# A pool of five PSUM banks, first inverses by quarters, and an order planned in both directions, in a DeltaNet kernel with a mixture-of-depths block

## The chip, the cores and the metric

The kernel runs on one core of a Trainium2 chip. Its time is the time of one execution on the device in microseconds (us); smaller is better. TensorE (PE in the profile) multiplies matrices and writes only to PSUM; VectorE (DVE), ScalarE (ACT) and GpSimd (POOL) work element by element, and SyncE (SP) issues most of the DMAs. [...]

## The reference

Attention block: batch 4, 8 heads, 768 steps, head width 48. For each batch and head a state of 48x48 starts at zero, and per step, with k normed:

```
y[t]   = q[t] @ state
v_old  = state^T @ k[t]
state += beta[t] * outer(k[t], v[t] - v_old)
```

The heads' outputs side by side are x, of 4 x 768 x 384. Mixture of depths: score = x @ w_gate; in each batch the 128 rows with the highest score get `x + sigmoid(score) * (relu(x @ w1) @ w2)`, with w1 of 384x1024 and w2 of 1024x384; the other rows stay x.

## The kernel before, in words

**Chunks.** The recurrence is done in chunks of C = 64 steps. Two batches form a group, so a unit holds 16 pairs of batch and head; 12 chunks by 2 groups give 24 units, numbered i. Inside a chunk the recurrence becomes a triangular system, whose inverse is needed once for each unit and head.

**Preparation of a unit** (`prep`): k and q are loaded, turned by TensorE (`turn`, L460), copied out by ScalarE (L464), then the products k k^T (`products_g`, L479) and q k^T (`products_p`, L489) are made and copied out (L496, L503; each product lies in two banks and is copied in two parts), and `mask_p` (L511, POOL) masks the second.

**Elimination** (`eliminate`), once for four units (a set e, 0 to 5): the 64x64 triangle of each head is two 32x32 blocks on the diagonal and one below. VectorE turns the diagonal blocks so that each partition holds one whole block of 1024 elements (`turn_in`, L580), scales it, ScalarE copies it to PSUM (`fill`, L615), and 30 steps of two instructions each (`step`, L624 multiplies, L628 subtracts) invert it; then `final` (L634), `turn_out` (L640) and `turn_back` (L646). `join` puts the two inverted blocks and the block below together with two TensorE products per unit, z (L691) and j (L703), and copies on ScalarE (L697, L709).

**Recurrence of a unit** (`recur`), the serial part: V (`mm_v`, L755) puts v into PSUM through the identity; R (`mm_r`, L741) adds state times k; ScalarE copies it (L759); W (`mm_w`, L767) applies the inverse; ScalarE copies the two halves (L772); S (`mm_s`, L780) updates the state in its own bank and ScalarE copies it (L786). Outputs: Q (`mm_q`, L796) and Y (`mm_p`, L807), copied in two parts (L814), stored, weighed (L824) and summed to scores (L830).

**Depths** (`depths`), once per batch: ranks by comparison, chosen rows gathered by an indirect DMA, first product (`mm_1`, L1051), second (`mm_2`, L1065), an indirect DMA that adds into the output (L1074). Their products stand after the last W in the order of TensorE.

**PSUM.** Eight banks: three single ones called inv (turned k and q, products, z, j, Y, depths), two for the elimination (pa), a fixed pair `prec` that V, R and W of all units share, one for the state (psta).

**Order.** `Plan` holds each piece of work as an `Op` with an engine, an assumed duration, what it waits for and which buffers (rings) it takes and gives back. `order` walks forward in assumed time and lets the engines pick; `rank` runs it once and then sets each priority to the length of the tail behind the piece. `fill` puts short bf16 matmuls of ones (`filler`, L1161; one call issues two) where it thinks TensorE would stand idle. The result fixes each engine's sequence when the program is built.

Of the kernel before, what the change touches and what calls it, by code (L numbers as in the profile page):

```python
# [17 lines left out]
HC = 32  # L18

# [6 lines left out]
class Plan:  # L26
# [30 lines left out]

    def pick(self, free, ops):
# [3 lines left out]
        for t, op in sorted(ops, key=lambda x: (x[1].prio, x[1].seq)):  # L62
            at, need = max(free, t), {}
            for name, _ in op.take:
                need[name] = need.get(name, 0) + 1
            if kept & set(need):
                continue
            late = {n: sorted(self.rings[n])[k - 1] for n, k in need.items()}
            held = [n for n in late if late[n] > at]
            if held and t <= free + 0.3 and held == ["inv"]:  # L70
                kept.add("inv")
            at = max([at] + list(late.values()))
            if at < float("inf"):
                cand.append((at, op))
# [40 lines left out]
    def order(self):  # L115
# [6 lines left out]
        while len(done) < len(self.ops):  # L122
# [10 lines left out]
            for name, key in op.take:  # L133
                slots = self.rings[name]
                k = min(range(len(slots)), key=lambda x: slots[x])
                slots[k] = float("inf")
                self.slot[key] = (name, k)
# [17 lines left out]
    def rank(self):  # L155


        slots, refs = {n: len(s) for n, s in self.rings.items()}, dict(self.refs)
        self.order()
        givers, then, held, tail = {}, {}, {}, {}  # L160
# [3 lines left out]
        for op in sorted(self.ops, key=lambda o: (o.start, o.seq)):  # L164
            for name, key in op.take:
                if name != "inv":
                    for g in givers.get(held.get(self.slot[key]), []):
                        then.setdefault(g.seq, []).append(op)
                    held[self.slot[key]] = key
        for op in sorted(self.ops, key=lambda o: (o.end, o.seq), reverse=True):  # L170
            tail[op.seq] = op.dur + max(
                [tail[u.seq] + (op.lat if u.eng != op.eng else 0.0) for u in op.users] +
                [tail[u.seq] + 0.15 for u in then.get(op.seq, []) if u.seq in tail] + [0.0])
        for op in self.ops:
            hot = op.prio < -500 and op.eng != "PE"
            op.prio = -tail[op.seq] - (1000 if hot else 0)
            op.left, op.start, op.end = len(op.deps), None, None
        self.refs, self.slot = refs, {}
        for n, c in slots.items():
            self.rings[n] = [0.0] * c  # L180
# [18 lines left out]
def kernel(  # L199
# [63 lines left out]
    KF = F // P  # L263
    PSUM = bass.MemoryType.PSUM
# [21 lines left out]
    ring("a", 2, [HC * HC])  # L286
# [6 lines left out]
    ring("cmp", 2, [22 * P], BF16)  # L293
# [3 lines left out]
    rings["inv"] = [psum.tile([P, 512], FP32, name=f"inv{m}") for m in range(3)]  # L297
    plan.ring("inv", 3)
    rings["A"] = [psum.tile([P, HC, HC], FP32, name="pa")]
    plan.ring("A", 1)  # L300
    prec = psum.tile([P, 2, 512], FP32, name="prec")
    pfull = psum.tile([P, 512], FP32, name="psta")
    psta = pfull[:, :GI * 2 * D].rearrange("p (r d) -> p r d", d=2 * D)

# [41 lines left out]
    later = sbuf("later", [C])  # L346
    base = sbuf("base", [NT])
# [20 lines left out]
    wbd = [sbuf(f"wbd{m}", [GP, 2, D]) for m in range(2)]  # L368
    sts = [sbuf(f"s{m}", [GI, 2, D]) for m in range(2)]
# [6 lines left out]
    def constants():  # L376
# [10 lines left out]
        for t in wbd:  # L387
            nc.vector.memset(t, 0.0)
        for t in rings["tt"]:
# [8 lines left out]
    def late_constants():  # L398
# [4 lines left out]
        for b in range(B):  # L403
# [7 lines left out]
            nc.gpsimd.tensor_copy(tok[b][:, :, 0, 1], own[b])  # L411

# [43 lines left out]
    def turn(i, nm):  # L456
# [6 lines left out]
        def out():  # L463
            nc.scalar.copy(got(nm + "T", i),  # L464
                           got("inv", i, nm).rearrange("p (r t) -> p r t", t=P))
# [28 lines left out]
    def split_g(i, rt):  # L494
        def emit():
            nc.scalar.copy(  # L496
                blocks(got(*gk(i // BC)), i % BC)
                .rearrange("p (k r) x t -> p k r x t", r=2)[:, :, rt], small(i, "g", rt))
        return emit

    def split_p(i, rt):
        def emit():
            nc.scalar.copy(  # L503
                got("p", i).rearrange("p (r b) t -> p r b t", b=2)[:, :, rt],
                small(i, "w", rt).rearrange("p a b t -> p (a b) t"))
# [22 lines left out]
    def shift0(i):  # L528

        def emit():  # L530
            left, right = lower(got(*gk(i // BC)), slice(i % BC * GP // 2,
                                                         (i % BC + 1) * GP // 2))
            for x in range(2):
                nc.vector.tensor_copy(right[lo[x]], left[lo[x]])
        return emit

    def prep(i):
# [3 lines left out]
        for nm in "kq":  # L541
            n["l" + nm] = moved(sp, 1.3, 1.15, load(i, nm), prio=u - 30 + (nm == "q") * 34,
                                take=[(nm, i)], lat=2.5)
        for nm in "kq":
# [5 lines left out]
            n["e" + nm] = act(0.6, put, [n["t" + nm]], v, give=[("inv", i, nm)])  # L550
        for w, v, made, deps, rate in (
                ("g", u, (products_g, split_g), [n["ek"], N[e * BC].get("g")], 1.2),
                ("w", u + 31, (products_p, split_p), [n["ek"], n["eq"]], 1.2)):
            keys = [("inv", i, w, rt) for rt in range(2)]
            n[w] = pe(0.71 if w == "g" else 0.5, made[0](i), deps + [N.get(i - 1, {}).get(w)], v, rate=rate,
                      take=keys + ([("p", i)] if w == "w" else
                                   [gk(e)] * (i % BC == 0)))
            for rt in range(2):
                n[w, rt] = act(0.37, made[1](i, rt), [n[w], n.get((w, 0))], v,
                               give=[keys[rt]])  # L560
        n["mp"] = pool(1.1, mask_p(i), [n["w", 0], n["w", 1], N["masks"]], 10 * i - 10)
        done = [n["g", 0], n["g", 1]]
        if i < BC:
            n["sh"] = dve(0.6, shift0(i), done, u)
# [5 lines left out]
    def eliminate(e):  # L570
# [3 lines left out]
        eng, on = (nc.vector, dve) if e == 0 else (nc.gpsimd, pool)  # L574

        def rows(t):
            return t.rearrange("p (i c) -> p i c", c=HC)

        def turn_in():
            nc.vector.transpose(  # L580
                out=rows(got("a", e)).rearrange("p t (n x) -> p t n x", x=2),
                in_=got(*gk(e))[:, :, HC:].rearrange("p n t x -> p t n x"))

        def square():
            eng.tensor_scalar_max(nrm[:, 0], got("a", e)[:, ::HC + 1], 1e-30)
# [17 lines left out]
        def clear():  # L603
            a = rows(got("a", e))
# [3 lines left out]
        def scale():  # L608
            a = rows(got("a", e))
            eng.tensor_tensor(out=a, in0=a, op=ALU.mult,  # L610
                              in1=bh[e % 2][:, :, None].to_broadcast([P, HC, HC]))
            eng.memset(got("a", e)[:, ::HC + 1], -1.0)

        def fill():
            nc.scalar.copy(got("A", e), rows(got("a", e)))  # L615

        def step(j):
            w = HC - 1 - j

            def emit():  # L620
                a = rows(got("a", e))
# [10 lines left out]
        def final():  # L632

            nc.vector.tensor_tensor(  # L634
                out=got("a", e).rearrange("p (i c x) -> p i x c", c=HC, x=2),
# [3 lines left out]
        def turn_out():  # L639
            nc.vector.transpose(  # L640
                out=got("tt", e)[:, :, HC:].rearrange("p n t x -> p t n x"),
                in_=got("a", e).rearrange("p (i c x) -> p i x c", c=HC, x=2))

        def turn_back():
# [3 lines left out]
                in_=got("a", e).rearrange("p (i c x) -> p c i x", c=HC, x=2))  # L648
# [16 lines left out]
        last = on(1.4 if e == 0 else 2.2, scale, [s["sc"], cl], -650 if e else u)  # L665
        last = act(1.0, fill, [last], -600, take=[("A", e)])
        for j in range(1, HC - 1):
            emit, dur = step(j)
            last = dve(dur, emit, [last, N.get(("e", e - 1), {}).get("tb")], u)
        s["fi"] = last = dve(1.25, final, [last], u, give=[("A", e)])  # L670
        s["to"] = last = dve(1.3, turn_out, [last], u, take=[("tt", e)])
        s["tb"] = last = dve(1.3, turn_back, [last], u, give=[("a", e)])
        for m in range(BC):
            s["mv", m] = pool(0.7, move(m), [s["to"]], -640)
        for m in range(BC):
            join(e, m)

    def join(e, m):
# [32 lines left out]
        n["z"] = pe(0.53, z, [s["to"]], u, rate=0.3, take=[key[0]])  # L711
        n["ez"] = act(0.4, ez, [n["z"]], u, give=[key[0]])
        n["j"] = pe(0.53, jj, [n["ez"], s["tb"]], u, rate=0.3, take=[key[1]], give=[gk(e)])
# [5 lines left out]
    def recur(i):  # L719
# [5 lines left out]
        wb, s_old, s_new = wbd[i % 2], sts[(i + 1) % 2], sts[i % 2]  # L725
        both_r = prec[:, :, :GP * D // 2]
# [8 lines left out]
        def mm_r():  # L735
            t = got("kT", i)
            pr = both_r.rearrange("p r (k b d) -> p r k b d", b=2, d=D)
# [454 lines left out]
```

## Time and profile before

| what | value |
|---|---|
| median of three runs | 314.7 us (313.43 to 322.67) |
| the profiled execution, its own time | 316.69 us |
| its span, first to last instruction | 314.9 us |
| mean granted TensorE clock | 0.933 of full speed |
| busy: PE, DVE, ACT, POOL | 280.6, 201.7, 176.1, 149.1 us |
| first W (unit 0), last W (unit 23) | start at 58.0 and 250.1 us |

A time in the profile is counted from the start of its span. A line of a timeline gives start, duration, engine, source line, operation, output and inputs with their sizes, count, and in brackets how long the engine stood idle before and who ended that. A line of the stretches gives, for one stretch of the span, its length, then each engine's busy time with its count of instructions, the granted clock of TensorE and the share of time in which the DMA engines worked. A product of two float32 operands is recorded as two passes, so 16 products show as x32.

### The profile page before, as it was taken

What the parts mean: (1) busy time and instruction counts of PE and PEld (TensorE: products, weight loads), DVE (VectorE), ACT (ScalarE), POOL (GpSimd) and SP (SyncE); (2) the same over time, 40 slices, a digit from 0 to 9 for tenths busy, and PEclk for the clock granted to TensorE, in tenths of its full rate; (3) what the DMA queues carried; (4) which work ended last, traced back from release to release, by engine and by line L of the source; (5) the groups of instructions that cost most, each with busy time, mean ns of one, the idle gap of its engine ahead of it and who ended that gap; (6) DMA issues with size and microseconds to landing.
All of it is one profiled execution on the core that took longest, in us unless ns stands there. A gap on an engine that the chain in (4) does not pass through costs nothing.

```text
span 314.9 us, 15794 instructions
## 1 busy us (share of the span) xinstructions
PE 280.6 (89%) x6930; PEld 230.8 (73%) x6930; DVE 201.7 (64%) x632; ACT 176.1 (56%) x453; POOL 149.1 (47%) x232
## 2 busy tenths in 40 slices
PE   5979539998999989989999898999999999999990
PEld 5868428777888768877878677777877877777770
DVE  7379966997799779997984259957335565642000
ACT  1766406666868768676568557775467851212210
POOL 7056687834744694377042974466133442212201
PEclk9997957999999999997589999998599999999996
DMA  5776797265425343566223532435210211112012
GB/s 102 140 132 121 163 167 160 42 123 108 98 58 113 89 93 75 97 126 168 54 53 76 103 80 55 104 81 151 48 34 11 61 41 49 11 41 27 25 25 25
DMA packets 87923, 26.21 MB, mean 83 GB/s; under 512 B 82448, under 2 KB 87280, under 8 KB 87856
## 3 DMA queue, kind: packets, MB, share of 16 engines
q1 hardware_dynamic: 86256, 23.54, 35.1%
q0 software_dynamic: 1600, 1.68, 3.3%
q8 instruction: 54, 0.88, 1.1%
q14 instruction: 13, 0.11, 0.1%
HBM read 18.38 MB, written 5.51 MB: 76 GB/s over the span
## 4 chain that ended last, share of the span: by engine, by line
PE 65%; DVE 11%; ACT 8%; issue 5%; DMA 5%; POOL 3%; SPq 1%; POOLq 1%; DVEq 0%; ACTq 0%
PE inv L807 5%; PE inv L1051 5%; PE inv L460 5%; PE psta L780 5%; PE inv L1065 5%; PE prec L755 5%; PE prec L767 4%; PE psta L1161 4%; PE inv L796 4%; PE inv L703 4%; PE prec L741 3%; PE inv L691 3%; DVE pa L628 3%; DVE tmp L624 3%; PE inv L489 3%
## 5 line engine op out<-in xcount | busy, mean ns | idle before, releaser
L624 DVE TENSOR_TENSOR tmp<-a,pa 128x30 f32<-128x30 f32 (+9 forms) x180 | 58.6, 326 | 17.1 <-ACT pa L615 11.4
L628 DVE TENSOR_TENSOR pa<-pa,tmp 128x30 f32<-128x30 f32 (+9 forms) x180 | 60.8, 338 | 6.2
L824 POOL TENSOR_TENSOR xw<-x,wg 128x384 f32<-128x384 f32 x23 | 23.1, 1002 | 42.1 <-ACT x L814 23.8
L511 POOL TENSOR_TENSOR p<-p,later 128x512 f32<-128x512 f32 x24 | 30.3, 1271 | 16.2 <-ACT p L503 15.7
L731 POOL TENSOR_TENSOR v<-v,nnT 128x384 f32<-128x384 f32 x24 | 19.9, 829 | 34.1 <-DMA v<-in_v_dram 30.3
L1161 PE MATMUL psta<-warm 128*128 128x128 bf16 x242 | 27.7, 241 | 3.8 <-DVE psta L385 3.8
L772 ACT COPY wbd<-prec 64x384 f32<-64x384 f32 x48 | 22.7, 472 | 13.9 <-PE prec L767 12.5
L1051 PEld LDWEIGHTS inv<-xeT,w_sb 128*128 128x128 f32 x192 | 24.0, 192 | 5.1 <-ACT xeT L1045 0.9
L1065 PE MATMUL inv<-w_sb,hT 128*128 128x384 f32 x64 | 25.4, 498 | 0.3 <-ACT hT L1058 0.3
L1051 PE MATMUL inv<-xeT,w_sb 128*128 128x128 f32 x192 | 25.3, 279 | 0.2 <-ACT xeT L1045 0.2
L780 PE MATMUL psta<-wbd,k 128*48 128x96 f32 x352 | 20.3, 261 | 5.2 <-ACT wbd L772 4.9
L460 PE MATMUL inv<-ident,q 128*128 128x128 f32 x96 | 16.7, 307 | 7.7 <-DMA q<-in_q_dram 7.7
L807 PE MATMUL inv<-wbd,p 128*64 128x96 f32 x384 | 23.0, 267 | 0.2 <-POOL p L511 0.2
L479 PE MATMUL inv<-kT 48*64 48x64 f32 x768 | 20.2, 230 | 2.9 <-ACT g L496 2.6
L1161 PEld LDWEIGHTS <-warm 128*128 128x128 bf16 x242 | 17.5, 107 | 6.8 <-issue 2.6
L780 PEld LDWEIGHTS psta<-wbd,k 128*48 128x48 f32 x352 | 15.8, 129 | 8.7 <-ACT wbd L772 8.1
L1058 ACT ACTIVATE hT<-inv 128x256 f32<-128x256 f32 x16 | 6.1, 383 | 26.5 <-PE inv L1051 26.5
L479 PEld LDWEIGHTS inv<-kT 48*64 48x64 f32 x768 | 16.2, 140 | 6.3 <-ACT g L496 3.8
L709 ACT COPY tt<-inv 32x256 f32<-32x256 f32 x48 | 18.5, 385 | 4.2 <-PE inv L703 3.3
L755 PE MATMUL prec<-v,ident 128*128 128x192 f32 x88 | 20.7, 360 | 0.0
L1074 POOL DMA_INDIRECT out_dram<-xe,idx x4 | 6.4, 1594 | 29.6 <-ACT xe L1070 29.6
L654 POOL COPY tt<-tt 32x256 f32<-32x256 f32 x48 | 18.8, 391 | 2.9 <-DVE tt L640 0.8
(127 smaller groups left out, 589.9 us busy)
## 6 DMA issues: line engine op xcount, KB each, us to landing
k<-in_k_dram SPq DMA_DIRECT2D x48, 96.0 KB
v<-in_v_dram SPq DMA_DIRECT2D x48, 96.0 KB
q<-in_q_dram SPq DMA_DIRECT2D x48, 96.0 KB
out_dram<-x SPq DMA_DIRECT2D x24, 192.0 KB
w_sb<-in_moe_w_dram SPq DMA_DIRECT2D x3, 512.0 KB
w_sb<-in_moe_w_dram SPq DMA_DIRECT2D x4, 384.0 KB
g<-g SPq DMA_DIRECT2D x16, 64.0 KB
bt<-in_beta_dram POOLq DMA_DIRECT2D x24, 4.0 KB, 3.0
```

What stands on the lines that cost most here:

```text
L460: nc.tensor.transpose(ps[:, r * P:(r + 1) * P], x[:, 2 * r:2 * r + 2].rearrange("p b d -> p (b d)"), ident)
L479: nc.tensor.matmul(small(i, "g", rt)[half[bb], k, par], lhsT=x, rhs=x, start=True, stop=True)
L511: nc.gpsimd.tensor_tensor(out=t, in0=t, op=ALU.mult, in1=later[:, None, :].to_broadcast([P, GP, C]))
L624: nc.vector.tensor_tensor(out=t, op=ALU.mult, in0=a[:, j + 1:, j:j + 1].to_broadcast([P, w, j]), in1=x[:, j:j + 1, :j].to_broadcast([P, w, ...
L628: nc.vector.tensor_tensor(out=x[:, j + 1:, :j], in0=x[:, j + 1:, :j], in1=t, op=ALU.subtract)
L755: nc.tensor.matmul(pv[:, rt], lhsT=ident, rhs=heads(got("v", i))[:, rt], start=True, stop=False, skip_group_check=True)
L780: nc.tensor.matmul(psta[ds[a % 2], a // 2], lhsT=t[:, a, :D], rhs=wb[:, a].rearrange("p h d -> p (h d)"), start=(c == 0 and a < 2), stop=True,
L807: nc.tensor.matmul(y(rt)[half[bb], k].rearrange("p b d -> p (b d)"), lhsT=t[:, a], rhs=wb[:, a].rearrange("p h d -> p (h d)"), start=(c == ...
L824: nc.gpsimd.tensor_tensor(out=got("xw", i), in0=got("x", i), op=ALU.mult, in1=wg)
L1051: nc.tensor.matmul(got("inv", b, "h", f // 2)[:, f % 2 * CAP:(f % 2 + 1) * CAP], lhsT=w1_sb[:, t, f * P:(f + 1) * P], rhs=got("xeT", b)[:, ...
L1065: nc.tensor.matmul(got("inv", b, "o")[:CAP, :DM], lhsT=got("hT", b)[:, f], rhs=w2_sb[:, f], start=(f == 0), stop=(f == KF - 1))
L1161: nc.tensor.matmul(pfull[:, GI * 2 * D:], lhsT=warm, rhs=warm, start=False, stop=True, skip_group_check=True)
```

## The change

Five things are changed together.

1. **One pool.** The three inv banks and the pair `prec` become one tile of five banks, `invs`. V and R take two neighbouring banks of it, W takes two others, and so do Q with Y, and the products of keys. `room` finds the neighbouring banks that come free first. A product in two banks is now copied out by one instruction in place of two (`split`, `out_x`).
2. **More buffers in the recurrence.** Three of `wbd` and three of the state copies stand in place of two each. With a pair of banks of its own, V of the next unit is no longer made to wait for the copies of W and for S.
3. **Quarters for set 0** (`PARTED = (0,)`). The 32x32 blocks of the first set are inverted as two 16x16 quarters at once (`step_q`, 14 steps), and `join_q` puts the quarters together on TensorE: for each of the four units zq (an identity product and 32 small products), a copy, jq (32 products), a copy, uq (16 products that turn the result back), a copy. Only then do z and j follow. The other sets are inverted as before.
4. **Moved work.** The copies of the first four turned k go from ScalarE to VectorE; the shifts of set 0 (`shift0`) from VectorE to POOL; clearing of `tt` and the tokens' constants to later places on POOL. The batch of 12 k loads is followed by q before v on SP.
5. **The planner** (`rank`) repeats 90 turns of a forward walk (`order`) and a backward one (`latest`), with noise after turn 20, and keeps the order whose assumed end is first. In the new order 164 filler matmuls stand where there were 242.

```
-    rings["inv"] = [psum.tile([P, 512], FP32, name=f"inv{m}") for m in range(3)]
-    plan.ring("inv", 3)
+    invs = psum.tile([P, 5, 512], FP32, name="invs")
+    rings["inv"] = [invs[:, m] for m in range(5)]
+    plan.ring("inv", 5)
-    prec = psum.tile([P, 2, 512], FP32, name="prec")
+    def beside(keys):
+        m = plan.live[keys[0]][1]
+        return invs[:, m:m + 2]
...
+    def room(self, name, count):
+        s = self.rings[name]
+        return min((max(s[k:k + count]), k) for k in range(len(s) - count + 1))
...
-            for rt in range(2):
-                n[w, rt] = act(0.37, made[1](i, rt), [n[w], n.get((w, 0))], v,
-                               give=[keys[rt]])
+            n[w, 0] = n[w, 1] = act(0.62, split(i, w), [n[w]], v, give=keys)
-            n["sh"] = dve(0.6, shift0(i), done, u)
+            n["sh"] = pool(0.7, shift0(i), done, -700)
...
+        def step_q(j):
+            w = QC - 1 - j
+            def emit():
+                a, x = quarter(got("a", e)), state()
+                t = tmp[:, :2 * w * j].rearrange("p (s i c) -> p s i c", s=2, c=j)
+                nc.vector.tensor_tensor(
+                    out=t, op=ALU.mult,
+                    in0=a[:, :, j + 1:, j:j + 1].to_broadcast([P, 2, w, j]),
+                    in1=x[:, :, j:j + 1, :j].to_broadcast([P, 2, w, j]))
+                nc.vector.tensor_tensor(out=x[:, :, j + 1:, :j], in0=x[:, :, j + 1:, :j],
+                                        in1=t, op=ALU.subtract)
+            return emit, 0.42 + 1.9e-3 * 2 * w * j
...
+        def z():
+            tt, ps, l = got("tt", e)[:, at], view("zq", QC), zq[:, at]
+            nc.tensor.matmul(got("inv", i, "zq")[:, :GP * QC], lhsT=identb,
+                             rhs=low_i.rearrange("p n t -> p (n t)"), start=True, stop=False,
+                             skip_group_check=True)
+            for f in range(GP):
+                for x in quad:
+                    nc.tensor.matmul(ps[x.start:x.start + QC, f // 2, f % 2],
+                                     lhsT=l[x, f // 2, :, f % 2],
+                                     rhs=tt[x, f // 2, HC + QC:, f % 2], start=False,
+                                     stop=True, skip_group_check=True)
...
+        n["zq"] = pe(0.75, z, [s["to"], s["kp"], N["quarters"]], u, rate=0.3, take=[("inv", i, "zq")])
+        n["ezq"] = act(0.4, ez, [n["zq"]], u, give=[("inv", i, "zq")])
+        n["jq"] = N["jq"] = pe(0.7, jj, [n["ezq"], s["tb"]], u, rate=0.3, take=[("inv", i, "jq")])
+        n["eq_j"] = act(0.4, ej, [n["jq"]], u, give=[("inv", i, "jq")])
+        n["uq"] = pe(0.5, back, [n["eq_j"]], u, rate=0.3, take=[("inv", i, "uq")])
+        n["euq"] = act(0.4, eb, [n["uq"]], u, give=[("inv", i, "uq")])
...
-            r["v"] = pe(0.75, mm_v, [r["vh"], o.get("s"), o["w0"], o["w1"]], u, rate=1.3,
-                        give=[("v", i)])
+                r["v"] = pe(0.75, mm_v, [r["vh"], o.get("w")], u, rate=1.3,
+                            give=[("v", i)], take=rk)
...
-        r["w"] = pe(0.5, mm_w, [x, n["ej"], o.get("w0"), o.get("w1")], u, rate=1.5,
+        r["w"] = pe(0.5, mm_w, [x, n["ej"]], u, rate=1.5, take=wk,
...
-        xo = None
-        for rt in range(2):
-            xo = act(0.37, out_x(rt), [r["p"], xo], 10 * i + 8, take=[("x", i)] * (rt == 0),
-                     give=[yk[rt]])
+        xo = act(0.5, out_x, [r["p"]], 10 * i + 8, take=[("x", i)], give=yk)
```

The planner's loop:

```
+        for turn in range(TURNS):
+            self.renew(slots, refs)
+            for op in self.ops:
+                op.prio = weight[op.seq] - hot[op.seq]
+            width = noise.choice((0, 0, 1, 2, 4)) if turn > 20 else 0
+            try:
+                self.order()
+                end = max(op.end for op in self.ops)
+                if best is None or end < best[0]:
+                    best = (end, weight)
+                weight = self.latest(turn % 2 == 0)
+            except RuntimeError:
+                weight, width = best[1], 2
+            weight = {q: t + noise.uniform(-width, width) for q, t in weight.items()}
```

## The prediction

> **What bounds the kernel now.** I read the page's first two parts, then the busy time by stretch, then the timelines of VectorE and TensorE in the stretches that differ.
>
> ```profile
> PE 280.6 (89%) x6930; PEld 230.8 (73%) x6930; DVE 201.7 (64%) x632; ACT 176.1 (56%) x453; POOL 149.1 (47%) x232
> PEclk9997957999999999997589999998599999999996
> ```
>
> TensorE is the busiest engine, but 11% is open, and its clock is down to half in three places. The stretches tell where the open time lies (length; busy time of PE, PEld, DVE, ACT, POOL; clock; share of the DMA engines):
>
> ```profile
> 3.00:58.00 55.00, 43.28 (x974) 37.14 (x973) 38.54 (x104) 26.92 (x66) 32.92 (x53) 0.88 0.74 141
> 58.00:250.00 192.00, 180.54 (x5453) 151.12 (x5451) 140.36 (x404) 131.06 (x344) 99.94 (x161) 0.94 0.38 85
> 250.00:308.00 58.00, 56.80 (x507) 42.48 (x505) 20.70 (x110) 16.49 (x43) 12.73 (x12) 1.00 0.15 31
> 146.00:160.00 14.00, 14.00 (x334) 12.16 (x332) 12.83 (x35) 5.79 (x15) 4.12 (x5) 0.51 0.34 95
> ```
>
> Three stages, then. Up to the first W at 58.0 TensorE has 11.7 us open, and much of its busy time is filler. From the first to the last W (250.1) 11.5 us are open. After the last W it has no more than 1.2 us open until its last product at 307.5; the last copy, the scatter and the end take the 7.4 us to 314.9. So 58.0 + 192.1 + 57.4 + 7.4 = 314.9.
>
> What ends the first stage is VectorE, the elimination of set 0:
>
> ```profile
> 15.61 1.25 DVE L580 STREAM_TRANSPOSE a<-g 128x1024 f32<-128x1024 f32 x1
> 21.95 0.20 DVE L624 TENSOR_TENSOR tmp<-a,pa 128x30 f32<-128x30 f32 x1 [1.08 <-ACT pa L615]
> 22.43 0.22 DVE L624 TENSOR_TENSOR tmp<-a,pa 128x58 f32<-128x58 f32 x1
> 23.50 0.27 DVE L624 TENSOR_TENSOR tmp<-a,pa 128x108 f32<-128x108 f32 x1
> 49.26 0.35 DVE L595 RECIPROCAL bh<-nrm 128x32 f32<-128x32 f32 x1 [4.78 <-POOL nrm L591]
> 51.27 1.25 DVE L640 STREAM_TRANSPOSE tt<-a 128x1024 f32<-128x1024 f32 x1
> ```
>
> The inverse is there at 52.5; z, j and copies need 5.5 us more. The 4.78 us are a wait for POOL, whose root on ScalarE stood behind q copies.
>
> TensorE's own prices, at full and at half clock:
>
> ```profile
> 53.17 0.70 PE L691 MATMUL inv<-tt,g 32*32 32x32 f32 x32
> 146.18 1.00 PE L691 MATMUL inv<-tt,g 32*32 32x32 f32 x32
> ```
>
> The last product's end is modelled, so I price a group from its start to the next group's start: z 0.63 us at full clock (53.17 to 53.80). In the same way turning (four products) 0.60, key products, R and Q 0.66, V 0.85, W 0.67, S 0.86, Y 0.81, and per f 0.67 and 0.65 in the two depth products. A ledger of all groups from first to last W at these prices gives 180 us, and the units at full clock agree with it within 0.9 us each (unit 5: 5.31 us measured, 5.8 in the ledger). The rest is the clock.
>
> **What the Trainium skill says.** "TensorE: Matmul & The Clock Gate", Part 1 (the HAM clock gate): the clock is either full or half, and falls after about one window of 3.4 us with little work. The trace agrees: 0.51 over 146 to 160, four such windows. It fell there in a row of z with fillers between. The same page, "Wait — 56ns, not 53.3ns?": starts come no closer than about 25 ns however small a product is. The trace has 32 passes in 0.63 us, 19.7 ns, so the measurement decides; I keep 25 only as an upper bound. "TensorEngine Tiling (Array Packing)", Key Properties: tiles of 32x32 work independently. z uses two of them in turn, zq and jq four; no row of this trace shows four. "PSUM — Partial Sum Buffer", Terms: TensorE and another engine must not be on one bank and quadrant at once; hence a pair of banks is held until its copy ends.
>
> **The change part by part.**
>
> *Set 0 on VectorE.* Starts of successive steps lie 0.24 us apart at 30 elements, 0.26 at 58, 0.31 at 108. The 14 steps on two quarters have 28 to 112 elements: 28 instructions at 0.29 make 8.1 us where 30 steps took 21.7 (21.95 to 50.0, less the wait and 1.6 of set 1's work): 13.6 less. Half the elements in scale and fill (1.23 and 1.02 now; a copy of 512 took 0.59): 1.0 less. The root of set 1 now stands ahead of the last masked product's copy and of the quarters' copies on ScalarE, so the 4.8 us wait goes. `final` in two parts and two memsets: nothing, 0.65 each way against 1.23. Against it: two more banks to clear (0.52 each), one more wbd (0.70), turned k copied behind them, shifts on POOL at 0.39 for 0.28: turn_in 1.4 later. The inverse is out at 52.5 - 13.6 - 1.0 - 4.8 + 1.4 = 34.5. Next late is the DMA shift of set 1, behind 24 k and 4 q issues of 0.7: about 28 us, just in time for its turn_in.
>
> *Joining quarters, all on the path.* Before the first W the new order has four identity products (0.1 each, an estimate from a bf16 filler), four zq and four jq of 32 products, three uq and three z and two j at 0.63, and 17 filler calls at 0.22. A zq costs 0.63 if four tiles give twice z's rate, 1.26 at z's rate, 1.6 at the page's floor (64 passes); I take 1.0. Sum 0.4 + 8.0 + 5.0 + 3.7 = 17.1 (14.1 to 21.9). Copies (0.3 each) lie beside the next group. Small products hardly load the array and the clock was already half from 42 to 50: I add 1.0. First W at 34.5 + 17.1 + 1.0 = 52.6, that is 5.4 earlier. Of 18 us won on VectorE, TensorE's joins give back 12.6.
>
> *Sets 1 to 5.* Set 1's fill is queued on ScalarE behind the four zq copies: steps from about 41.5 rather than 54.6. This doesn't shorten the middle, as TensorE is full there; it only takes away waits.
>
> *The middle.* From the order, first to last W now holds 4 more turnings, 3 masked-product groups, a Q, a Y, a uq, a j, a rank spread (1.05), a turning of gathered rows (0.5) and 10 counts (0.6), and 24 filler calls less: 2.4 + 2.0 + 1.5 + 1.3 + 2.2 - 5.3 = +4.1. Copies in one part: some 57 pairs after the first stage lose about 0.17 each (two at 0.38 against one of 0.59), 10 us of ScalarE's 131. TensorE waited on ScalarE some 12 us in all; I take 2 of them back. The half-clock stretches (about 25 us in the middle, work 1.6 times slower, so 9.4 us lost) I leave as they are. Middle 192.1 + 4.1 - 2 = 194.2.
>
> *The end.* What moved ahead of the last W leaves it: Q, Y, spread, turning, counts, 3.6. So 57.4 - 3.6 = 53.8. The tail of 7.4 stays. Third wbd and state buffers, POOL's moved constants and `keep` (0.8 beside ScalarE's fill) cost nothing: POOL is idle half the time; without that cover clearing tt (1.9) would delay turn_in's successor by 1.9.
>
> Sum 52.6 + 194.2 + 53.8 + 7.4 = 308.0 against 314.9, 6.9 less. The profiled execution took 316.69 (1.8 around its span), the median 314.7; I subtract the difference from the median: 307.8.
>
> **The rivals.**
>
> *The clock stays full.* The planner's search packs TensorE more tightly and the 9.4 us go: 298.4. For: fewer gaps. Against: fewer fillers, and it takes W at 0.5 where the trace has 0.67, so its idea of the load is too high. 20%.
>
> *The joins eat the gain.* Half clock through the quarters (z went from 0.63 to 1.0) and zq at the page's floor: 21.9 x 1.3 is 28.5, first W at 63.0, 10.4 later than forecast; at 1.26 and full clock 2.1 later. 310 to 318, likeliest 314. For: 19 us of small products with 17 filler calls, whereas 8 calls from 140.7 to 146.2 did not hold the clock. 20%.
>
> *Slower: pairs in one pool.* Five banks hold two pairs at most; V and R keep one for some four us, so W, Q with Y, and two products take turns on the other, and a single bank in use can split it. If V/R or W (46 groups on the path) meet a pair whose copy is still running, each loses up to 0.48 (the copy at L772): 22 us. It decides from 0.29 each on, 13.3 us, where 2% slower (321) is passed; at two thirds 322.5. For: prec was free of all others. Against: the number of banks is as before, and these lines show how little TensorE waited:
>
> ```profile
> PE psta L780 <- ACT wbd L772: 4.9, 10, 0.8
> PE inv L479 <- ACT g L496: 2.6, 3, 1.7
> ```
>
> 14%.
>
> *The search changes nothing real* (its gain is in its own prices) is within my forecast, which credits it with 2 us.
>
> **How the numbers follow.** Forecast 46% (303 to 313, 307.8), full clock 20%, joins 20%, pairs 14%. About 2% is what this measurement can tell from no change: below 308.4 is faster. Half of the forecast's share and a little more, with the full clock's, gives 0.47; the pairs give slower 0.14; the rest is 0.39. The range leaves out the pairs and a quarter of the full clock: 299 to 320.
>
> **What would show it.** Right: first W at 50 to 55, tt written at about 34.5, a zq group of 0.6 to 1.3 us, last W at 247. Wrong: half clock between 35 and 55; a growing wait of TensorE before V and W on ScalarE; the last W before 240. Most likely to make it wrong is the clock, whose stretches I can't place.

## The result, and the profile after

The changed kernel takes 592.6 us (median of four runs, 583.83 to 602.19) where the kernel before takes 315.0: the ratio is 1.865, with a 95% interval of 1.842 to 1.888. The forecast was 307.8. Here and below the ratios leave disturbed runs out on both sides, so that they can differ from the quotient of the medians beside them.

The page of the profiled execution (602.19 us, span 600.2), its busy time, clock and chain:

```profile
PE 435.1 (72%) x7496; PEld 342.3 (57%) x7496; DVE 186.5 (31%) x602; ACT 171.8 (29%) x389; POOL 153.9 (26%) x247
...
PEclk9555655555555565555555555555565575676998
...
PE 67%; ACT 20%; issue 7%; DVE 2%; POOL 2%; DMA 1%; POOLq 0%; SPq 0%; ACTq 0%; DVEq 0%
```

VectorE, ScalarE and POOL work about as long as before. TensorE has 8% more passes, yet its busy time grew by 154.5 us (280.6 to 435.1), and the span grew by 285.3, so its open time grew by the other 130.8. The clock is at half almost throughout. In the chain ScalarE has 20% in place of 8%.

The loss is in no one stage. The busy time by stretch, cut at the first W, the last W and the end (length; PE, PEld, DVE, ACT, POOL; clock; share of the DMA engines):

```profile
3.00:89.70 86.70, 59.72 (x1413) 47.72 (x1413) 40.29 (x108) 21.57 (x46) 34.98 (x66) 0.57 0.39 81
89.70:503.30 413.60, 304.29 (x5674) 245.37 (x5674) 124.71 (x374) 135.75 (x309) 105.95 (x166) 0.52 0.19 42
503.30:600.20 96.90, 71.08 (x422) 49.13 (x415) 19.41 (x106) 13.04 (x32) 10.92 (x10) 0.80 0.10 18
```

The middle, 192.1 us before, is about 413. Set 0's 28 steps on VectorE take 8.8 us (38.2 to 47.1, with 1.2 of set 1's work among them), as short as forecast, but all about them is late: from `turn_in` to tt it takes 23.5 us where the forecast has 17.5 (VectorE's timeline; L676 is `turn_in` and L783 writes tt):

```profile
26.10 1.25 DVE L676 STREAM_TRANSPOSE a<-g 128x1024 f32<-128x1024 f32 x1 [5.67 <-POOL g L626]
...
48.34 1.25 DVE L783 STREAM_TRANSPOSE tt<-a 128x1024 f32<-128x1024 f32 x1
```

**What the engines wait for.** ScalarE's and TensorE's waits in the profile after (in all us, times, longest):

```profile
ACT wbd L992 <- PE invs L553: 13.9, 8, 2.3
ACT x L1033 <- PE invs L987: 13.4, 6, 4.1
ACT r L978 <- PE invs L553: 10.9, 5, 4.2
PE psta L1000 <- ACT wbd L992: 12.7, 20, 1.1
```

The first three make no sense as data: the copy of W's result waits for a turning of k or q, the copy of an output for W, the copy of R for a turning. They have only the tile `invs` in common. The first microseconds show one such link after another (timelines of ScalarE, VectorE and TensorE):

```profile
11.71 0.61 ACT L592 COPY g<-invs 128x512 f32<-128x512 f32 x1 [9.40 <-PE invs L553]
...
12.35 0.69 DVE L558 COPY kT<-invs 128x512 f32<-128x512 f32 x1 [2.20 <-ACT g L592]
...
13.09 1.12 PE L553 MATMUL invs<-ident,k 128*128 128x128 f32 x4 [1.42 <-DVE kT L558]
...
17.29 0.61 ACT L592 COPY g<-invs 128x512 f32<-128x512 f32 x1 [4.97 <-PE invs L572]
...
17.95 1.11 PE L553 MATMUL invs<-ident,k 128*128 128x128 f32 x4 [0.73 <-ACT g L592]
```

In the program as built, each wait can be followed to the instruction that releases it. For these lines (banks counted 0 to 4):

```
ACT L592 copies banks 1,2   waits for PE  L553, which writes bank 3
DVE L558 copies bank  3     waits for ACT L592, which reads banks 1,2
PE  L553 writes bank  4     waits for DVE L558, which reads bank 3
ACT L592 copies banks 0,1   waits for PE  L572, which writes bank 3 last
```

Of ScalarE's 233 waits for TensorE, at least 166 are of this kind: the two instructions share the tile and no bank. (How many exactly depends on whether one counts the instruction that releases or its whole group.) So are at least 158 of TensorE's waits for ScalarE, 16 of its 57 for VectorE, and 18 of VectorE's waits for ScalarE, in which both are copies that only read. In the kernel before there are none.

**Theory.** The framework that writes the waits follows a PSUM tile as a whole. Made into one tile, the five banks allow one engine at a time: product, copy, product, copy. TensorE stands open during the copies, and the half clock comes with that. **Rival.** The small products of the joins and the fewer fillers hold the clock at half, and the rest follows from that.

### The profile page after: what moved, and what is told of

The parts are those of the page before. It is cut to its first block, busy times and chain, and to the rows that moved or that the text cites. A ratio compares the mean times of both kernels' runs of the same rounds, so it can differ in the third digit from the quotient of the medians.

```text
span 600.2 us, 16838 instructions
## 1 busy us (share of the span) xinstructions
PE 435.1 (72%) x7496; PEld 342.3 (57%) x7496; DVE 186.5 (31%) x602; ACT 171.8 (29%) x389; POOL 153.9 (26%) x247
## 4 chain that ended last, share of the span: by engine, by line
PE 67%; ACT 20%; issue 7%; DVE 2%; POOL 2%; DMA 1%; POOLq 0%; SPq 0%; ACTq 0%; DVEq 0%
PE invs L553 8%; PE invs L970 6%; PE invs L1027 6%; PE psta L1000 6%; PE invs L1270 5%; PE invs L582 4%; PE invs L987 4%; PE invs L572 4%; PE invs L901 4%; PE invs L1016 4%; ACT wbd L992 4%; PE invs L913 4%; PE invs L955 4%; PE invs L1284 4%; ACT tt L919 2%
## 5 line engine op out<-in xcount | busy, mean ns | idle before, releaser
L1027 PE MATMUL invs<-wbd,p 128*64 128x96 f32 x384 | 36.0, 364 | 13.3 <-ACT tt L919 2.9
L970 PE MATMUL invs<-v,ident 128*128 128x192 f32 x88 | 35.7, 561 | 4.5 <-ACT wbd L992 2.7
L1027 PEld LDWEIGHTS invs<-wbd,p 128*64 128x64 f32 x384 | 29.5, 217 | 16.4 <-issue 12.6
L1270 PE MATMUL invs<-xeT,w_sb 128*128 128x128 f32 x192 | 34.0, 332 | 6.5 <-ACT hT L1277 2.6
L1270 PEld LDWEIGHTS invs<-xeT,w_sb 128*128 128x128 f32 x192 | 30.2, 235 | 13.8 <-ACT hT L1277 4.6
L1000 PEld LDWEIGHTS psta<-wbd,k 128*48 128x48 f32 x352 | 26.4, 196 | 20.3 <-ACT wbd L992 19.9
L553 PE MATMUL invs<-ident,k 128*128 128x128 f32 x96 | 26.2, 426 | 13.2 <-ACT kT L558 3.0
L582 PE MATMUL invs<-qT,kT 48*64 48x64 f32 x768 | 26.6, 313 | 10.5 <-ACT p L596 3.0
L572 PE MATMUL invs<-kT 48*64 48x64 f32 x768 | 25.9, 309 | 10.9 <-ACT g L592 3.4
L1284 PE MATMUL invs<-w_sb,hT 128*128 128x384 f32 x64 | 28.5, 562 | 6.0 <-ACT hT L1277 2.7
L553 PE MATMUL invs<-ident,q 128*128 128x128 f32 x96 | 26.0, 426 | 6.9 <-ACT qT L558 2.1
L676 DVE STREAM_TRANSPOSE a<-g 128x1024 f32<-128x1024 f32 x5 | 6.2, 1245 | 78.9 <-DMA g<-g 54.7
```

The costliest lines, as they stand in the source:

```text
L553: nc.tensor.transpose(ps[:, r * P:(r + 1) * P], x[:, 2 * r:2 * r + 2].rearrange("p b d -> p (b d)"), ident)
L572: nc.tensor.matmul(small(i, "g", rt)[half[bb], k, par], lhsT=x, rhs=x, start=True, stop=True)
L582: nc.tensor.matmul(small(i, "w", rt)[half[par], r // 2, r % 2], lhsT=t[ds[rt], r, half[par]], rhs=s[ds[rt], r, half[par]], start=True, sto ...
L970: nc.tensor.matmul(pv()[:, rt], lhsT=ident, rhs=heads(got("v", i))[:, rt], start=True, stop=False, skip_group_check=True)
L1000: nc.tensor.matmul(psta[ds[a % 2], a // 2], lhsT=t[:, a, :D], rhs=wb[:, a].rearrange("p h d -> p (h d)"), start=(c == 0 and a < 2), stop=True,
L1027: nc.tensor.matmul(y(rt)[half[bb], k].rearrange("p b d -> p (b d)"), lhsT=t[:, a], rhs=wb[:, a].rearrange("p h d -> p (h d)"), start=(c == ...
```

## Experiments

`e2_before_one_tile`, `e4_after_fillers`, `e7_late_weights`, `e8_three_in_one` and `e11_half_jq` were executed once each.

**Five tiles in place of one** (`e1_five_tiles`), the planned order untouched:

```
-    invs = psum.tile([P, 5, 512], FP32, name="invs")
-    rings["inv"] = [invs[:, m] for m in range(5)]
+    rings["inv"] = [psum.tile([P, 512], FP32, name=f"inv{m}") for m in range(5)]
...
 def beside(keys):
-    m = plan.live[keys[0]][1]
-    return invs[:, m:m + 2]
+    return [got(*key) for key in keys]
...
-            nc.scalar.copy(heads(rhs[i % 2]), pv())
+            for rt in range(2):
+                nc.scalar.copy(heads(rhs[i % 2])[:, rt], pv()[rt])
```

(and in the same way the copies of W, Q with Y, and the key products.)

> The changed kernel in the same planned order, with its five banks as five tiles of one bank each in place of one tile of five; a product in two banks is copied out by one instruction for each bank. Theory (the tile of five banks is waited for as a whole, so that each TensorE group waits for the last copy out of any bank and each copy for the last group into any bank): the waits between different banks go, and the steps of the prediction hold roughly: 300 to 325 us, TensorE busy near 280 and open near 35 us, clock above 0.85, first W near 52. Rival (the small products of the joins and the fewer fillers hold the clock at half): still above 450 us with a clock below 0.65.

320.9 us against 312.8 for the kernel before, ratio 1.027 (1.014 to 1.041). Its page and its stretches:

```profile
PE 277.2 (88%) x7496; PEld 229.9 (73%) x7496; DVE 190.1 (61%) x602; ACT 178.1 (57%) x531; POOL 155.0 (49%) x247
...
PEclk9999655599799989999999999999999999999997
```

```profile
3.00:60.50 57.50, 43.47 (x1412) 36.97 (x1411) 40.45 (x107) 22.52 (x62) 34.34 (x65) 0.76 0.59 122
60.50:253.90 193.40, 181.34 (x5646) 152.10 (x5642) 128.36 (x375) 139.72 (x428) 106.47 (x166) 0.97 0.40 89
253.90:306.30 52.40, 52.40 (x444) 40.76 (x442) 19.23 (x106) 13.81 (x39) 10.64 (x9) 1.00 0.16 33
```

TensorE has the same 7496 passes, joins and fillers included, and they take 277 us in place of 435. That alone refutes the rival. 272 of the 278 us lost are gone, although ScalarE now has 142 instructions more. What the tile did to the clock shows here too: the mean is 0.934 where it was 0.573. Only the first W, at 60.5, is far from what I expected.

**The kernel before with one tile** (`e2_before_one_tile`), the opposite edit:

```
-    rings["inv"] = [psum.tile([P, 512], FP32, name=f"inv{m}") for m in range(3)]
+    five = psum.tile([P, 5, 512], FP32, name="five")
+    rings["inv"] = [five[:, m] for m in range(3)]
-    prec = psum.tile([P, 2, 512], FP32, name="prec")
+    prec = five[:, 3:5]
```

> The kernel before with its three inv banks and the pair prec as views of one tile of five banks; order, copies and all else are those of the kernel before. Theory: this alone does most of the damage, 450 to 620 us, clock below 0.7, TensorE's open time above 100 us. Rival (the joins, the fewer fillers or the new order did it): 313 to 318 us, as before.

581.4 us, from this edit alone:

```profile
PE 432.3 (75%) x6930; PEld 335.0 (58%) x6930; DVE 198.8 (34%) x632; ACT 178.1 (31%) x453; POOL 150.0 (26%) x232
...
PEclk9555566555555555655555559555565555678599
```

TensorE is open for 147 us, and the clock is down to 0.583. No join by quarters, no new order, no single filler less is needed for it. So the tile is the cause of both parts of the loss, open time and half clock.

**Three of the five in one tile** (`e8_three_in_one`): the kernel before with `rings["inv"]` as three views of one tile, `prec` apart.

> The kernel before with its three inv banks as views of one tile of three banks; the pair prec, the order and the copies stay as they were. Theory (waiting goes by tile, so that the damage grows with what shares the tile): V, R, W and S keep their own tiles and only the preparation, joins, outputs and depths wait for each other, 370 to 500 us. Rival (the damage comes from V, R and W sharing a tile with the rest): below 330 us.

437.5 us, about half of the way:

```profile
PE 353.9 (81%) x6930; PEld 277.6 (64%) x6930; DVE 199.4 (46%) x632; ACT 176.0 (40%) x453; POOL 149.6 (34%) x232
...
PEclk9655556599569956985775558986697556997997
```

V, R and W need not be in the shared tile. With them in it, in five banks, the damage is about twice as large.

**Two pairs and a single** (`e3_two_pairs_one`): the changed kernel with two tiles of two banks and one of one; `room` gives pairs only whole tiles, and copies stay in one part. With the new rule in `room` the order is planned anew.

> The changed kernel with its five banks as two tiles of two banks and one tile of one bank; a pair is always one whole tile, single banks go by preference to the tile of one, and pairs are still copied out in one part. Theory: a single product that sits in one half of a pair tile still waits for the other half, so between the two: 310 to 360 us, clock 0.75 to 0.93. Rival (joins and fillers): above 450 us.

329.2 us, ratio 1.045 (1.031 to 1.059). That is where my theory had it. The interval overlaps that of the five tiles. So two unlike users in a tile cost at most a few per cent here, and copies in one part win nothing that shows; as the order differs too, the run gives no price for either by itself. It also clears the copies in two parts of `e1_five_tiles` of having been the remedy.

**Fillers into the waits** (`e4_after_fillers`): the changed kernel with

```
+            if op.eng == "PE" and op.rate < 1.55 and not open_s:
+                filler()
+                filler()
             op.emit()
```

> The changed kernel with its one tile of five banks, and four filler matmuls more ahead of each group of TensorE (not between S and its copy), so that TensorE has work while it waits. It separates the two terms of the loss, 154 us of longer busy time and 131 us of open time. Theory: the waits stay and the clock rises to 0.8 or more, 420 to 520 us. Rival (the half clock is the cause and the waits its consequence): 320 to 370 us.

564.1 us; both forecasts missed, the rival's by far more. The page, and the fillers in the profile after and in this one:

```profile
PE 450.7 (80%) x8628; PEld 359.1 (64%) x8628; DVE 185.9 (33%) x602; ACT 172.0 (31%) x389; POOL 153.9 (27%) x247
...
PEclk9965655555688567999876895997769975899998
```

```profile
L1384 PE MATMUL psta<-warm 128*128 128x128 bf16 x164 | 25.0, 303 | 3.8 <-DVE psta L465 3.8
```

```profile
L1389 PE MATMUL psta<-warm 128*128 128x128 bf16 x1296 | 150.4, 257 | 4.0 <-DVE psta L470 3.8
```

The mean clock rose from 0.573 to 0.778, and the span fell by only 38 us. That does not make the clock a small matter. Without the fillers TensorE's busy time fell from 410 to 300 us (435.1 less 25.0, 450.7 less 150.4), but the fillers themselves take 125 us more, and the open time fell by only 54. The fillers stand in the queue between a wait and the next group, so most of them didn't fit into the waits and came on top. The run doesn't divide the loss cleanly into clock and waiting.

**Without quarters** (`e5_no_quarters`, and again in five rounds, `e9_no_quarters_5`): `e1_five_tiles` with `PARTED = ()`.

> The kernel of five one-bank tiles with set 0 inverted in 30 steps as the other sets are, without quarters and their joins; the order is planned anew. It prices the third part of the change. In the kernel with quarters the first W started at 60.5 us, where the kernel before had 58.0. Theory (the joins on TensorE give back all that VectorE gains): first W at 57 to 61 us and the same time within 1.5%, 311 to 321 us. Rival (the quarters still save the 5.4 us of the prediction): first W near 66 us, 321 to 329 us.

> The same kernel as in the no-quarters run (five one-bank tiles, set 0 inverted as the other sets), in five rounds, to tell whether it beats the kernel before. In the first run it had 315.2 us beside 317.5. Theory (what is left of the change, that is more buffers, the pool in single banks and the search, takes TensorE's waits out of the middle, where 187.7 us lay between first and last W in place of 192.1): 1 to 2.5% faster, ratio 0.975 to 0.99. Rival (that difference was the clock of one execution): ratio 0.99 to 1.01.

First 315.2 us beside 317.5, then 308.8 beside 317.4, ratio 0.993 (0.983 to 1.003). With quarters the ratio was 1.027: in this layout the kernel with them is some 3% slower. The first W is at 58.7 and 59.2 us, hardly earlier than with them (60.5), as my theory had it. Most of the difference is in the middle, 185.8 us in place of 194.2 in the second run (both counted to the last product of the last W), in an order that was planned anew; how much of it is due to the quarters stays open. Whether this kernel beats the one before is not settled: the interval includes 1, and 0.993 lies in the range of the rival (0.99 to 1.01), just outside the 0.975 to 0.99 that I expected. By its median it is the fastest of the changed kernels.

**One turn of the search** (`e10_one_turn`): the same with `TURNS = 1`.

> The no-quarters kernel with the planner's search cut from 90 turns to the first. It prices the search. Theory (the search orders the middle better): 1 to 3% slower than the kernel with 90 turns, 318 to 325 us beside its 315. Rival from the prediction (the search's gain is in its own prices): within 1% of it.

326.4 us, ratio 1.042 (1.025 to 1.059), against 0.993: the search is worth some 5%, more than the 1 to 3% that I expected. The middles of the two (`e9_no_quarters_5`, then `e10_one_turn`):

```profile
59.20:245.00 185.80, 175.69 (x5417) 148.19 (x5417) 130.57 (x387) 134.37 (x410) 97.09 (x150) 0.95 0.39 88
```

```profile
63.10:260.20 197.10, 185.65 (x5458) 155.06 (x5459) 138.28 (x401) 136.16 (x413) 96.79 (x134) 0.91 0.37 83
```

11 of the 15 us between the spans are here, nearly all as longer busy time at a lower clock; 4 are ahead of the first W.

**The old PSUM layout** (`e6_own_pair`, and without quarters `e12_own_pair_30`): a fixed pair for V, R and W and three single tiles, with all other parts of the change.

```
-    rings["inv"] = [psum.tile([P, 512], FP32, name=f"inv{m}") for m in range(5)]
+    rings["inv"] = [psum.tile([P, 512], FP32, name=f"inv{m}") for m in range(3)]
+    prec = psum.tile([P, 2, 512], FP32, name="prec")
+    rings["pair"] = [prec]
...
-        rk, wk = ([("inv", i, w, x) for x in range(2)] for w in ("r", "u"))
+        rk, wk = ([("pair", i, w)] for w in ("r", "u"))
```

> The changed kernel with the PSUM layout of the kernel before: a fixed tile of two banks for V, R and W of all units and three tiles of one bank for the rest; quarters, moved work, more buffers and the planner's search stay. It leaves out the pool. Theory (once the shared tile is gone, the pool of five is worth little either way): 310 to 320 us, within 1.5% of the kernel of five one-bank tiles. Rival (pairs of free banks shorten the middle, so that the old layout loses it): above 322 us. Second rival (the pool of single banks is what still costs 2%): below 310 us.

> The PSUM layout of the kernel before (a fixed tile of two banks for V, R and W, three tiles of one bank) without quarters, with the search, the third buffers and the moved work. The run with the old layout and quarters took 348 us, but 20 us of its middle went into one place where a v load stood late on SyncE's queue, so it did not price the layout. Theory (the layout is worth little): 306 to 314 us, ratio to the kernel before 0.98 to 1.01, like the kernel of five one-bank tiles without quarters (0.993). Rival (two free pairs let the middle run without V waiting for the copies of W, so that the old layout is slower): 316 us or more, ratio above 1.01.

348.4 us (336.75 at the lowest), and 320.8 without quarters, ratio 1.023 (1.000 to 1.046). Both are on the side of the rival. The middles and, for `e12_own_pair_30`, the stretch after the last W:

```profile
57.40:271.20 213.80, 192.50 (x5885) 161.10 (x5888) 129.68 (x380) 139.50 (x364) 108.59 (x159) 0.92 0.37 81
```

```profile
61.10:243.50 182.40, 168.72 (x5359) 142.97 (x5361) 134.46 (x395) 129.32 (x339) 94.06 (x139) 0.96 0.40 88
243.50:312.40 68.90, 58.81 (x579) 44.30 (x571) 21.63 (x115) 18.49 (x47) 16.60 (x15) 0.98 0.16 33
```

With quarters the middle is some 20 us longer than in `e1_five_tiles`, as the rival has it. Without them it is 182.4 us, shorter than that of any other run, which speaks against the rival; the loss is after the last W, 68.9 us against 62.2 in `e9_no_quarters_5`. There the chain goes through a scatter (4.38 us) and a gather (3.01) that stand one behind the other. My sentence on one place in the middle of `e6_own_pair` was a misreading: TensorE worked for 24.5 of those 27.0 us. Each layout is planned anew and gets its own order, so these runs don't price the layout by itself. That stays open.

**The stops inside the joins** (`e7_late_weights`, `e11_half_jq`). What was left in `e1_five_tiles` is the first W, 8 us late. TensorE's timeline shows the tile tt written in time, and then rows that stop in their midst for "issue", which is no wait that the profile knows:

```profile
34.10 0.72 PE L851 MATMUL inv<-tt,zq 32*16 32x16 f32 x64 [2.57 <-DVE tt L782]
...
38.05 0.30 PE L851 MATMUL inv<-tt,zq 32*16 32x16 f32 x14 [2.04 <-issue]
...
42.05 0.35 PE L851 MATMUL inv<-tt,zq 32*16 32x16 f32 x22 [1.49 <-issue]
...
47.25 0.52 PE L863 MATMUL inv<-zq,g 32*32 32x16 f32 x25 [3.01 <-issue]
...
50.70 0.62 PE L863 MATMUL inv<-zq,g 32*32 32x16 f32 x31 [0.50 <-issue]
```

That is 7.0 us. Between stops lie 128, 127 and 128 recorded passes, fillers counted. Each pass is a load and a product, so that makes 256 instructions. A packet of the instruction queue has 16384 bytes in the trace, which would be 64 for each of 256. In the trace such packets ended at 36.67, 40.40, 45.78 and 49.34, and TensorE went on 1.4 to 1.7 us after each. In all, 59 packets stand against 14992 loads and products, 254 to a packet. `e7_late_weights` issues the three w1 loads after unit 1's W:

> The kernel of five one-bank tiles with the three DMA issues of w1 (512 KB each) after unit 1's W on SyncE's queue and not before unit 0's; each other engine's order is unchanged. In the kernel of five tiles TensorE stood still four times inside the rows of zq and jq, 2.0, 1.5, 3.0 and 0.5 us, each time exactly 128 passes after the last stop, and each stop ended some 1.4 us after the end of a 16 KB packet of the instruction queue. Theory (TensorE is out of instructions there, and the packet that brings the next 256 comes later when the DMA engines are full of w1): the stop of 3.0 us falls to 1.0 to 1.8, the others stay within 0.5, first W at 58 to 59.5 us. Rival (the stops have nothing to do with the loads): the stop of 3.0 stays above 2.5 us.

```profile
40.49 0.30 PE L857 MATMUL inv<-tt,zq 32*16 32x16 f32 x14 [2.04 <-issue]
...
45.59 0.35 PE L857 MATMUL inv<-tt,zq 32*16 32x16 f32 x22 [2.58 <-issue]
...
49.69 0.52 PE L869 MATMUL inv<-zq,g 32*32 32x16 f32 x25 [1.91 <-issue]
...
53.69 0.62 PE L869 MATMUL inv<-zq,g 32*32 32x16 f32 x31 [1.05 <-issue]
```

The stops are at the same passes (14, 22, 25, 31), as one expects if TensorE runs out of instructions there. But their sum is 7.6 us, no less than 7.0. The third stop, where the w1 loads had been, fell from 3.0 to 1.9, short of the 1.8 I asked for; the second grew by 1.1 and the fourth by 0.55, where I had expected no more than 0.5. From 44 to 54 us the DMA engines were busy for at most 6% of each stretch of 2 us, and the last two stops, 3.0 us together, lie there. So traffic alone does not make the stops; a part of the third may have been due to it. The first W came at 63.5, not at 58 to 59.5, and from the first zq it took 26.9 us. (The execution took 328.7 us, its clock in the middle 0.91 where `e1_five_tiles` had 0.97.)

`e11_half_jq` leaves out half of the jq products of set 0 (`range(GP // 2)`):

> The kernel of five one-bank tiles in which each jq row makes only the first half of its products (16 of 32), so half of the quarters' blocks of set 0 stay as they were; all else and the order are the same. 128 passes fewer on TensorE, one packet of the instruction queue. From the start of the first zq to the first W the full kernel took 26.4 us, and 26.9 with the late w1 loads. Theory (these rows run at the rate at which instructions arrive, 128 passes in some 4 us): 3.2 to 4.5 us less, 22 to 23.4. Rival (they run at the rate of the products, 64 passes in 1.05 us at half clock): 2.1 us less at most, 24.2 or more.

From first zq to first W it took 24.6 us, 1.8 less than 26.4; the execution took 319.5. That is the rival's number. Three stops are left, 7.2 us together (2.38, 1.77, 3.06). The stop that went had been the small one of 0.5. So the stops at packets stand as observed; that a pass less saves a packet's share of time is not borne out, and what makes the stops as long as they are stays open.

The third buffers (part 2 of the change) and the moved work (part 4) were not run by themselves, so that nothing here prices them.

## Why the prediction was wrong

The step that failed is the price of the shared banks. The forecast's own sum put it at nothing: its middle, 192.1 + 4.1 - 2 = 194.2, has no term for a group that waits for a bank it does not use, and the first and last stages have none either. Measured were 89.7, about 413 and 96.9 us, where the sum has 52.6, 194.2 and 61.2. The rival "Slower: pairs in one pool" saw the right place, banks shared by V, R, W and the rest, but priced a wait of at most 0.48 us at 46 groups, 22 us in all, because it let a group wait only for a copy out of its own banks. It rested on what the Trainium skill states in "PSUM — Partial Sum Buffer", Terms, that two engines must not be on one bank and quadrant at once (no run here tests that), and on the claim that "the number of banks is as before". What counts is the number of tiles: these five banks were four tiles and became one. The waits are written by tile, and that edit alone took the kernel before to 581 us. The reading of TensorE's small waits in the profile before, 4.9 and 2.6 us, was right and of no use: it priced waits that existed, not those that the new tile adds. The diff showed `invs` as one tile, and the program as built holds the waits; which instruction each wait names was not asked.

With the tile split, the other steps can be compared one by one (`e1_five_tiles`):

| step | predicted | measured |
|---|---|---|
| tt written | 34.5 us | 33.96 |
| a zq group | 1.0 (0.63 to 1.6) | 0.65 |
| first zq to first W, joins and clock | 18.1 | 26.4 |
| first W | 52.6 | 60.5 |
| first to last W | 194.2 | 193.4 |
| last W to last product | 53.8 | 52.4 |
| tail | 7.4 | 7.3 |
| sum | 308.0 | 313.6 |

- *Elimination.* `turn_in` starts at 17.1 us (17.0 expected); the 13.6 us of steps and the 4.8 us wait went as worked out.
- *Joins.* Mis-sized by 8.3 us: 7.0 are the stops for instructions, which the sum had no term for. zq itself was cheaper than taken: its 64 passes take 0.65 us at half clock, about 10 ns for each, where z's 32 took 1.0. The upper bound of 1.6 was far too high.
- *Clock.* Half from about 33 to 64 us, as I feared. From there to the last W its mean is 0.98, better than the 0.94 I left in. The prediction says that the profile before agrees with "little work" ahead of a fall. It shows the two levels, half and full, and bears that out only in part: in the 3.4 us ahead of the falls at 23.4 and 40.5 us TensorE was recorded busy for 1.7 and 0.5, but ahead of those at 146.3 and 218.0 for 2.65 and 2.97.
- *Middle.* Right partly by luck: the clock was better than assumed, and yet the time came out as forecast. TensorE's open time is 12.1 us (11.5 before), so the 2 us I credited to copies in one part were not there, in a kernel that copies in two parts.
- *Search.* I credited it with 2 us and gave a rival the case that it changes nothing. It is worth about 15 in the kernel without quarters, measured against a single turn.

The rival "the joins eat the gain", with first W at up to 63 and 310 to 318 us, comes nearest to `e1_five_tiles`: first W at 60.5 and 315.6 us in the profiled execution, though its median of 320.9 lies above that range. The changed kernel as it was never got there, since the tile cost some 280 us first.

## What to carry to other kernels

Ask of every merged buffer what it is waited for by: a PSUM tile of several banks with unlike users is one lock, and the profile shows it as waits between instructions that share a name and no data. Split it into tiles that match what is written and read together, even at the price of one more copy instruction for each. And when small products are packed into rows, count instructions beside nanoseconds.

## What was unexpected of the hardware

- A row of 64 passes on four tiles takes 0.65 us (zq, 32*16) or 0.98 (jq, 32*32) at half clock, and in these rows TensorE stopped for 0.5 to 3.1 us about each time 128 passes had gone by. In the kernel with the late loads, packets of the instruction queue ended 4.4 and 4.0 us apart with the DMA engines all but idle. In no trace of this case did two of the 54 to 68 packets end less than 3.1 us apart. What sets that pace wasn't found.
- With TensorE waiting in turns with ScalarE, 1132 filler passes more, four ahead of each of 283 groups, raised the mean clock from 0.573 to 0.778 and not to full.
